# A relu moved forward on ScalarE, ahead of the lower sum that reads it, in a fused convolution and MLP kernel

## The chip, the cores and the metric

The kernel runs on one core of a Trainium2 chip. Its time is the device time of one execution in microseconds (us). Before the change it is 1008.81 us, the median of three runs (1006.14 to 1009.62).

## What is computed

The input x has 8 sequences of 4224 rows with 192 channels, all float32. First comes a causal convolution with 7 taps along the sequence; the 192 channels are 8 heads of 24, and each head has its own 7 weights, which are a softmax over the taps. Then an MLP block with a residual:

```python
w = softmax(weight)                        # (8 heads, 7 taps)
y = einsum('hk,bskhg->bshg', w, x_unfolded)   # y: (8, 4224, 192)
mu, var = mean(y), mean((y - mu) ** 2)     # over the 192 channels
yn = (y - mu) / sqrt(var + 1e-6) * g_ln
out = y + maximum(yn @ w_ch1, 0) @ w_ch2   # w_ch1: 192 x 768, w_ch2: 768 x 192
```

The kernel folds g_ln and the subtraction of the mean into the first weights, and since a positive factor passes through a relu, it multiplies by 1/sqrt(var) only after the second product.

## The kernel before

**Groups and stages.** The rows are cut into 18 groups. Groups 3 to 17 hold 16 rows on each of 128 partitions and are called mixed; a mixed group is one stage of the main loop. A stage does the first product with its relu (`up_mixed`) and then the second product (`down_fast`). Beside it, VectorE computes the convolution taps of the next group (`taps_of_next`, line 408), ScalarE the first two taps of the group after that (lines 383 and 394), and the output of the group before is scaled on ScalarE (`scale`, line 871, one row block j of 128 by 192 at a time) and added to memory by a DMA. The programs of the engines are in the order in which this file issues instructions; there is no reordering by a planner.

**A product in seven.** Both matrix products of a mixed group are done by Strassen's scheme in Winograd's form: the two operands are cut into quarters, and seven quarter products (with sums before and after) stand for eight. The hidden result has quarters c11, c12 (upper) and c21, c22 (lower).

**up_mixed.** The hidden dimension has 6 chunks of 128, three in each half. The pass is done for two sets of chunks: `one`, the small set (one chunk, index PAIR = 2), and `two` (two chunks, indices 0 and 1). Two sets of four PSUM banks, X and Y, take turns. In pass `two`, the line numbers and the order are these. `p.product` is TensorE (line 521). `p.evict` is ScalarE copying a bank set to the tile in SBUF, named room in the profile (line 616). `p.close(c, banks, part)` adds a bank set to a quarter: with a part, ScalarE copies the banks to the part (tiles parts_cs and parts_tb, or unused pieces of room) and a DMA from the GpSimd queue adds it (line 583, room<-parts_cs, room<-parts_tb, room<-room); without one, VectorE adds it directly (line 622). In the last stage all closes are VectorE's. `p.relu` is ScalarE in place (line 629).

The products accumulate: Y holds a11 b11, then s2 t0 on top of it (evicted as c21), then s1 b12, then s4 b22 (evicted as c12); X holds a12 b21, then s3 t1 (evicted as c22), then a22 t2, which `p.close(p.c21, X)` adds to c21 on VectorE. A product that follows an eviction or a close of the same banks waits for it.

**The lower sum.** `lower_sum` (line 767) is VectorE's in-place max(c21, 0) - c11, a first sum for the second product; it reads the relu of c11, chunk by chunk. It is called for chunk PAIR before `p.close(p.c21, X)`, and for the other two chunks after it.

**down_fast.** Seven products (line 791) of 36 matmuls, each recorded as two, in three column chunks c. The six banks are the next ones in turn, the four of X and two of Y. ScalarE copies finished chunks out (line 797), and after each copy it takes `behind` items from the list `work`: the relu of c22 of `one`, the scales, the two half relus of c22 of `two`, which the third product reads, and after them the first two taps of the group after next. `half_sum` (line 758) is VectorE's sums between the products. After them come the moments of the next group (line 439) and its sums (GpSimd lines 575 and 576, VectorE 578 and 579). In every second stage `root` then does the reciprocal square root on GpSimd (lines 457 to 470), in front of the next DMAs of the GpSimd queue.

Of the kernel before, what the change touches and what calls it, by code (L numbers as in the profile page):

```python
# [16 lines left out]
def kernel(  # L17
# [567 lines left out]
    def up_mixed(g, ahead):  # L585
# [9 lines left out]
        done = groups[g - 1][2]  # L595
# [40 lines left out]
        def act_scales(j1, j2):  # L636
            if not last:
                scale(g - 1, j1, j2)
# [7 lines left out]
        one, two = Pass(PAIR, FC, X, Y), Pass(0, PAIR, Y, X)  # L646
# [32 lines left out]
                add_to_out(g - 1, j1, j1 + HJ)  # L679
        p.product(Y, s2, p.t[0], False, False)  # L680
        p.evict(Y, p.c21)
        act_scales(1, 2)
        p.product(X, s3, p.t[1], True, False)
        p.evict(X, p.c22)
        act_scales(2, 3)
        p.product(Y, s1, p.b12, False, False)
        taps_of_next(2, 5)
        taps_of_next(5, 6, heads=(0, H // 2))
        p.close(p.c22, Y, rooms[1][:, 0:PAIR])
        act_scales(3, 4)  # L690
        p.product(X, a22, p.t[2], False)
        one.relu(one.c11)
        p.relu(p.c11)
        lower_sum(g, (PAIR,))
        p.close(p.c21, X)
# [11 lines left out]
        work = [lambda: one.relu(one.c22)]  # L707

        def scale_one(j):
            scale(g - 1, j, j + 1)  # L710
            if j == 7:
                add_to_out(g - 1, 0, 8)
            elif j == done - 1:
                add_to_out(g - 1, 8, done)

        if not last:
            work += [lambda j=j: scale_one(j) for j in range(4, done)]
        half = [lambda i=i: two.relu(two.c22[:, i : i + 1]) for i in range(PAIR)]
        return work[0:11] + half + work[11:]

    po = {}

# [146 lines left out]
    def scale(g, j1, j2):  # L869
        for j in range(j1, j2):  # L870
            nc.scalar.mul(ots[g][:, j, :], ots[g][:, j, :], rstd[g][:, j : j + 1])  # L871

    def add_to_out(g, j1, j2):
        if groups[g][0] is None:

            j1, j2 = (0, j2) if j2 == groups[g][2] else (0, 0)
        for ps, rows in rows_of_out(g, j1, j2) if j2 else ():
            nc.gpsimd.dma_start(  # L878
                out=rows, in_=ots[g][ps, j1:j2].rearrange("p j d -> p (j d)"), accum_op=ALU.add
            )  # L880
# [55 lines left out]
    def ahead(g):  # L936


        if results is not None:
            for half in range(2):  # L940
                finish_fast(g - 1, half, *results)
        yield

    for g in range(NG):
# [3 lines left out]
        if mixed:  # L948
            work = up_mixed(g, ahead(g))
        else:  # L950
            up(g)
# [73 lines left out]
```

## Time and profile before

| | busy us | share of the span |
|---|---|---|
| TensorE matmul | 958.6 | 95% |
| VectorE | 903.3 | 90% |
| ScalarE | 683.7 | 68% |
| GpSimd | 271.4 | 27% |

The profiled execution spans 1005.1 us; the granted TensorE clock is 0.996 of full speed. A stage in the middle, from the start of its second product to that of the next stage, takes 58.01 us (from 560.28 to 618.29); in it TensorE is busy for 55.95 us, VectorE 52.99, ScalarE 43.35 and GpSimd 12.45, and the DMA engines for a share of 0.77. The stage before, which has a `root` in front of its first product, takes 58.46.

The rows of the profile in the next parts are read as follows. PE is TensorE, DVE is VectorE, ACT is ScalarE and POOL is GpSimd. A timeline row has the start and the length in us, the engine, the line, the operation, the tile written and the tile read, the shapes and a count; what stands in brackets is how long the engine was idle before it, and what released it. Several like instructions can be merged into one row. Matmul ends are modelled.

### The profile page before, as it was taken

To read this page: it belongs to the slowest core of one execution; us is meant where nothing else is said; L and a number is where in the kernel's file an instruction comes from. 1 tells how busy PE (TensorE), PEld (TensorE's weight loads), DVE (VectorE), ACT (ScalarE), POOL (GpSimd) and SP (SyncE) were. 2 spreads that over 40 slices of the span, in tenths; PEclk is the share of its full clock that TensorE was granted. 3 is DMA by queue.
4 is the path that set the end of the run, shared out by engine and by line. 5 is a ranking of instruction groups with operands and counts; after the bars stand their busy time and mean duration, and the time that the engine had idled before them with its cause. 6 is when DMAs were issued, how large, how long until landed. Compare 5 with 4: busy or idle time off the path is not lost.

```text
span 1005.1 us, 38307 instructions
## 1 busy us (share of the span) xinstructions
PE 958.6 (95%) x17274; PEld 732.5 (73%) x17274; DVE 903.3 (90%) x1491; ACT 683.7 (68%) x1098; POOL 271.4 (27%) x383
## 2 busy tenths in 40 slices
PE   7999999999999999999999999999999899998997
PEld 6887586766869586776868677686867668595787
DVE  6999989979898998989899898989999798989757
ACT  5626577586877869586776958677695867775361
POOL 2004313513144221712135131523117121342200
PEclk9999999999999999999999999999999999999999
DMA  8252978478696877679787785878777796855031
GB/s 197 93 168 88 203 187 238 86 160 235 125 269 125 236 152 183 172 150 267 141 235 143 197 196 112 254 147 240 144 209 150 143 264 128 189 108 106 2 65 66
DMA packets 26386, 165.15 MB, mean 164 GB/s; under 512 B 3567, under 2 KB 4463, under 8 KB 18542
## 3 DMA queue, kind: packets, MB, share of 16 engines
q0 software_dynamic: 19120, 99.36, 50.6%
q1 hardware_dynamic: 6798, 63.34, 17.0%
q8 instruction: 135, 2.21, 0.9%
q14 instruction: 29, 0.24, 0.1%
q10 hardware_dynamic: 304, 0.00, 0.0%
HBM read 38.95 MB, written 50.33 MB: 89 GB/s over the span
## 4 chain that ended last, share of the span: by engine, by line
PE 58%; ACT 11%; DVE 10%; DMA 9%; POOL 6%; issue 5%; ACTq 0%; DVEq 0%; POOLq 0%
PE ps L521 31%; PE ps L791 21%; DVE room L758 7%; PE ps L738 5%; ACT room L629 5%; DMA room<-room 5%; ACT ot L871 4%; DMA room<-parts_cs 3%; DVE st L439 2%; ACT cs L797 2%; POOL d L457 2%; POOL d L467 1%; DMA xg<-in_x_dram 1%; ACT room L616 1%; POOL r L470 1%
## 5 line engine op out<-in xcount | busy, mean ns | idle before, releaser
L408 DVE SCALAR_TENSOR_TENSOR y<-xg,taps,y 128x384 f32<-128x384 f32 (+3 forms) x734 | 366.8, 578 | 0.2
L791 PE MATMUL ps<-room,w2sums 128*32 128x256 f32 (+1 forms) x4320 | 241.7, 377 | 8.1 <-ACT room L629 4.0
L521 PE MATMUL ps<-yt,w 32*128 32x256 f32 (+2 forms) x4104 | 238.6, 379 | 0.1
L616 ACT COPY room<-ps 128x1024 f32<-128x1024 f32 (+1 forms) x132 | 172.1, 1303 | 90.6 <-PE ps L521 80.6
L521 PEld LDWEIGHTS ps<-yt,w 32*128 32x128 f32 x4104 | 203.6, 185 | 27.7 <-issue 7.0
L791 PEld LDWEIGHTS ps<-room,w2sums 128*32 128x32 f32 x4320 | 146.4, 110 | 97.6 <-ACT room L629 17.1
L791 PE MATMUL ps<-room,w 128*32 128x256 f32 (+1 forms) x3240 | 181.6, 377 | 24.6 <-issue 21.7
L791 PEld LDWEIGHTS ps<-room,w 128*32 128x32 f32 x3240 | 111.8, 110 | 88.0 <-issue 32.0
L758 DVE TENSOR_TENSOR room<-room 128x1024 f32<-128x1024 f32 (+1 forms) x135 | 158.6, 1247 | 10.4 <-PE ps L791 10.4
L521 PE MATMUL ps<-ysums,w1sums 32*128 32x256 f32 x2160 | 123.8, 377 | 0.0
L521 PEld LDWEIGHTS ps<-ysums,w1sums 32*128 32x128 f32 x2160 | 110.5, 185 | 9.6 <-POOL v L458 1.8
L767 DVE SCALAR_TENSOR_TENSOR room<-room 128x1024 f32<-128x1024 f32 (+1 forms) x45 | 52.8, 1201 | 64.9 <-ACT room L629 63.5
L797 ACT COPY cs<-ps 128x256 f32<-128x256 f32 (+1 forms) x180 | 65.2, 365 | 65.7 <-PE ps L791 65.7
L871 ACT ACTIVATE ot<-ot,r 128x192 f32<-128x192 f32 x232 | 94.6, 455 | 0.0
L878 POOL DMA_DIRECT2D out_dram<-ot x40 | 34.3, 1079 | 209.6 <-ACT ot L871 131.1
L629 ACT ACTIVATE room<-room 128x1024 f32<-128x1024 f32 (+1 forms) x75 | 89.1, 1227 | 0.9 <-DMA room<-parts_cs 0.8
L383 ACT ACTIVATE y<-xg,taps 128x384 f32<-128x384 f32 (+3 forms) x141 | 74.1, 605 | 7.3 <-DMA out_dram<-y 6.9
L797 ACT COPY room<-ps 128x256 f32<-128x256 f32 (+1 forms) x90 | 33.4, 371 | 66.8 <-PE ps L791 66.8
L439 DVE BATCH_NORM_STATS2 st<-y 128x6 f32<-128x192 f32 x264 | 70.1, 341 | 0.0
L521 PE MATMUL ps<-yt,w1sums 32*128 32x256 f32 x1080 | 65.0, 379 | 2.3 <-ACT room L616 2.3
L521 PE MATMUL ps<-ysums,w 32*128 32x256 f32 x1080 | 64.8, 378 | 0.0
L394 ACT ACTIVATE tb<-xg,taps 128x384 f32<-128x384 f32 x112 | 60.3, 633 | 0.0
(103 smaller groups left out, 893.5 us busy)
## 6 DMA issues: line engine op xcount, KB each, us to landing
xg<-in_x_dram SPq DMA_DIRECT2D x15, 2112.0 KB, 15.9
out_dram<-ot POOLq DMA_DIRECT2D x29, 768.0 KB, 8.5
y<-tb POOLq DMA_DIRECT2D x28, 768.0 KB, 10.7
room<-room POOLq DMA_DIRECT2D x42, 512.0 KB, 5.7
out_dram<-y SPq DMA_DIRECT2D x13, 1536.0 KB, 8.0
room<-parts_cs POOLq DMA_DIRECT2D x14, 1024.0 KB, 8.5
room<-parts_tb POOLq DMA_DIRECT2D x14, 1024.0 KB, 6.9
xg<-in_x_dram SPq DMA_DIRECT2D x1, 1536.0 KB, 7.7
```

The costliest lines, as they stand in the source:

```text
L383: nc.scalar.mul(y[g][:, 0:n, cs], xg[g][:, 0:n, cs], taps[:, h, 0:1])
L394: nc.scalar.mul(tb[g][:, 0:n, cs], xg[g][:, 1 : 1 + n, cs], taps[:, h, 1:2])
L408: nc.vector.scalar_tensor_tensor(out=y[g][:, 0:n, cs], in0=t[:, k : k + n, cs], scalar=taps[:, h, k : k + 1], in1=y[g][:, 0:n, cs], op0=AL ...
L439: nc.vector.bn_stats(out=sums[g][:, j, :], in_=y[g][:, j, :])
L521: nc.tensor.matmul(banks[:, q, i * w : i * w + w], right[rows, c, P * i : P * i + P], left[rows, :, c, :], start=(first and c == 0 and i = ...
L616: nc.scalar.activation(dst, src, AF.Relu) if relu else nc.scalar.copy(dst, src)
L629: nc.scalar.activation(c, c, AF.Relu)
L758: nc.vector.tensor_tensor(a[:, *dst, f], a[:, *left, f], a[:, *right, f], op=op)
L767: nc.vector.scalar_tensor_tensor(out=a[:, 1, 0, f], in0=a[:, 1, 0, f], scalar=0.0, in1=a[:, 0, 0, f], op0=ALU.max, op1=ALU.subtract,)
L791: nc.tensor.matmul(dst[C * q : C * q + C, 0:w], right[:, f, C * c : C * c + C], left[:, f, q], start=(first and f == PAIR), stop=(f == PAI ...
L797: nc.scalar.copy(to[:, c], dst[:, 0:w].rearrange("p (j t) -> p j t", t=t))
L871: nc.scalar.mul(ots[g][:, j, :], ots[g][:, j, :], rstd[g][:, j : j + 1])
```

## The change

In `up_mixed`, the relu of the small set's upper left quarter, `one.relu(one.c11)`, moves from behind TensorE's last-but-one product to behind the c21 eviction of pass `two`, so that it is done before VectorE comes to the first lower sum. It takes the place of one scale of the group before; one more scale is taken out further down. These two scales (j = 2 and 3) are done in `down_fast` instead, at the head of its scales. There the half relus move from place 11 of the list to place 9, which is one copy sooner.

```diff
         p.product(Y, s2, p.t[0], False, False)
         p.evict(Y, p.c21)
-        act_scales(1, 2)
+        one.relu(one.c11)
         p.product(X, s3, p.t[1], True, False)
         p.evict(X, p.c22)
-        act_scales(2, 3)
+        act_scales(1, 2)
         p.product(Y, s1, p.b12, False, False)
         taps_of_next(2, 5)
         taps_of_next(5, 6, heads=(0, H // 2))
         p.close(p.c22, Y, rooms[1][:, 0:PAIR])
-        act_scales(3, 4)
         p.product(X, a22, p.t[2], False)
-        one.relu(one.c11)
         p.relu(p.c11)
         lower_sum(g, (PAIR,))
         p.close(p.c21, X)
...
         if not last:
-            work += [lambda j=j: scale_one(j) for j in range(4, done)]
+            work += [lambda j=j: scale_one(j) for j in range(2, done)]
         half = [lambda i=i: two.relu(two.c22[:, i : i + 1]) for i in range(PAIR)]
-        return work[0:11] + half + work[11:]
+        return work[0:9] + half + work[9:]
```

## The prediction

> **What bounds the kernel now.** First the busy shares of the page, which say whose time is being spent.
>
> ```profile
> PE 958.6 (95%) x17274; PEld 732.5 (73%) x17274; DVE 903.3 (90%) x1491; ACT 683.7 (68%) x1098; POOL 271.4 (27%) x383
> ```
>
> TensorE sets the pace, so a change counts only where TensorE stands still. Next, who waited for whom (waiter and line, what it waited for, total us, times, longest).
>
> ```profile
> DVE room L767 <- ACT room L629: 63.5, 14, 5.3
> PE ps L791 <- issue: 21.7, 14, 1.6
> PEld ps L791 <- ACT room L629: 17.1, 26, 0.8
> ```
>
> VectorE loses 63.5 us waiting for relus, in 14 stages: every mixed stage but the last. TensorE has 14 gaps of up to 1.6 us put down to "issue", so the profile names no cause. To find it I took one stage in order of time (start us, us, engine, line, operation), TensorE first.
>
> ```profile
> 611.33 2.77 PE L521 MATMUL ps<-yt,w1sums 32*128 32x256 f32 x48
> 613.91 2.77 PE L521 MATMUL ps<-ysums,w 32*128 32x256 f32 x48
> 618.29 4.09 PE L791 MATMUL ps<-room,w 128*32 128x256 f32 x72 [1.61 <-issue]
> 622.17 5.21 PE L791 MATMUL ps<-room,w2sums 128*32 128x256 f32 x88
> 627.69 3.23 PE L791 MATMUL ps<-room,w2sums 128*32 128x256 f32 x56 [0.31 <-ACT room L629]
> 630.74 4.07 PE L791 MATMUL ps<-room,w 128*32 128x256 f32 x72
> ```
>
> The first two rows are the last products of up_mixed, X with a22 and Y with s4; the rest are the first four of seven products of down_fast (72 records each), here P1 to P7. Starts tell more than the modelled ends. The step from 611.33 to 613.91 is 2.58, so P1 could have started at 616.49; it started at 618.29, 1.80 late. From P1 to P2 is 3.88; from P2 to P4 should be 7.76 and is 8.57, so the short wait inside P3 costs 0.81. It is in every mixed stage but the first and the last. Now VectorE and ScalarE in the same stretch.
>
> ```profile
> 595.36 14.87 DVE L408 SCALAR_TENSOR_TENSOR y<-xg,taps,y 128x384 f32<-128x384 f32 x28
> 614.77 1.22 DVE L767 SCALAR_TENSOR_TENSOR room<-room 128x1024 f32<-128x1024 f32 x1 [4.54 <-ACT room L629]
> 615.91 2.28 DVE L622 TENSOR_TENSOR room<-room,ps 128x2048 f32<-128x2048 f32 x1
> 618.29 2.36 DVE L767 SCALAR_TENSOR_TENSOR room<-room 128x1024 f32<-128x1024 f32 x2
> ```
>
> ```profile
> 606.39 1.87 ACT L616 COPY room<-ps 128x2048 f32<-128x2048 f32 x1 [0.37 <-PE ps L521]
> 608.15 0.46 ACT L871 ACTIVATE ot<-ot,r 128x192 f32<-128x192 f32 x1
> 609.02 1.87 ACT L616 COPY room<-ps 128x2048 f32<-128x2048 f32 x1 [0.41 <-ACT ot L871]
> 613.33 0.46 ACT L871 ACTIVATE ot<-ot,r 128x192 f32<-128x192 f32 x1
> 613.69 2.85 ACT L629 ACTIVATE room<-room 128x1024 f32<-128x1024 f32 x2
> 616.75 1.88 ACT L616 ACTIVATE room<-ps 128x2048 f32<-128x2048 f32 x1 [0.21 <-PE ps L521]
> ```
>
> VectorE is through with the taps at 610.23 and waits 4.54 for the first L629 relu (c11 of `one`) before the lower sum of L767. Behind that stands L622, close(c21, X), which reads bank set X; it ends at 615.91 + 2.28 = 618.19. P1 writes bank 0, which is in X, and starts at 618.29, 0.10 later. So I read the gap as ScalarE relu, lower sum, L622, TensorE. The last stage supports it: there the lower sum does not wait, and the gap is short and named (P1's start, and the L622 before it, which ends at 970.00):
>
> ```profile
> 970.14 2.89 PE L791 MATMUL ps<-room,w 128*32 128x176 f32 x72 [0.22 <-DVE room L622]
> 967.72 2.28 DVE L622 TENSOR_TENSOR room<-room,ps 128x2048 f32<-128x2048 f32 x1
> ```
>
> **What the Trainium skill says.** "Perfetto Trace Analysis", section "Per-instruction lifecycle: what the profiler-reported window actually captures", says ScalarE, VectorE and GpSimd are strict FIFOs and that TensorE's ends are estimated. The trace agrees: L622's product was over at 614.10, yet it ran at 615.91 behind L767; and I count TensorE's losses by starts. "PSUM — Partial Sum Buffer", section "Engine vs sequencer instructions", has the rule to guard PSUM by bank and quadrant; P1 waiting for the reader of X fits. "ScalarE: Activation LUTs", section "What ACT_TABLE_LOAD costs", gives 186 ns + 0.833 ns per element without pointer operands, an estimate of 1039 ns for 1024 elements; the trace has 1060 (median), which I use. "SBUF — State Buffer", section "Who interferes with whom", lets a VectorE instruction with two SBUF inputs block a GpSimd read. The trace agrees: GpSimd's L575 takes 1.84 at best and 3.44 in the median, beside L758.
>
> **The change part by part.**
>
> *1. Relu of c11 moved up.* It comes after the c21 eviction on ScalarE, in place of one scale: about 608.2 to 609.2. The lower sum then runs right after the taps, 610.3 to 611.5, and L622 waits for its product alone: 611.33 + 2.77 = 614.10, plus 0.14 (last stage: product end 964.57, L622 at 964.71) = 614.24, plus 2.28 = 616.52, plus 0.10: P1 at 616.62 instead of 618.29. Gain 1.67. VectorE's wait doesn't vanish: of 4.54 us, 2.8 become a wait for TensorE. In stages with a 1.45 gap (P1 at 560.28, product start 553.37 with an end of 556.24), P1 comes at 558.76, gain 1.52. The 21.7 us split into 9 of the first kind and 5 of the second: 9 x 1.67 + 5 x 1.52 = **22.6 us**.
>
> *2. What the early relu pushes.* Behind it on ScalarE stands the c22 eviction, and for that TensorE's X, a22 product waits. Before, it ran from 609.02; now the relu leaves it free at 608.15 + 0.96 = 609.12, ending at 610.99, while TensorE starts that product at 611.33. Cost 0, hidden by the Y, s1 product. The relu needs the first room<-room transfer. In stages after a `root`, GpSimd issues it late (540.65 in one) and transfers take 4.2 to 9.8 us: landing between 544.9 and 550.5, against a relu slot at 549.4. Even the slowest ends the relu at 551.46, and there the eviction waits for a later transfer until 551.45 anyway. Taken 0; upper end, were that later transfer early, 0.96 less the slack of 0.34 in 7 stages, 4.3 us.
>
> *3. Half relus one copy sooner, two more scales in down_fast.* The c12 eviction stays at 616.75 to 618.63, since TensorE sets it, so the first P1 copy starts near 618.6. ScalarE then runs without a pause at measured steps: copy 0.26, relu of c22 0.96, scale 0.35. Four copies (1.04), one relu, eight scales (2.8), half relu (0.96) and the second one's 1.06 end at 625.4. P3 reaches its last third at 616.62 + 7.77 + 0.86 = 625.25. So TensorE waits 0.16 instead of 0.81: 0.64 in 12 stages (the first had none; in g = 16 a wait for VectorE at 927.77, 2.63 long, swallows it) = **7.7 us**. The later scales delay taps and y<-tb by under 1 us; ScalarE's P5 copy came 1.6 us before P6 needed its bank, and y<-tb is read a stage later: 0.
>
> *4. What comes nearer.* (a) TensorE gains 0.64 inside P3, while VectorE's L758 sums, tied to L622, come only 0.2 earlier relative to P1. P5 needs three of them: 572.60 + 2 x 1.14 + 1.22 = 576.10 against 576.61 before; that slack goes. Estimate 0.05 in 13 stages, **0.7**. (b) In 7 stages the chain moments, root, room<-room, c22 eviction is late already (ScalarE waited up to 1.8 for it); TensorE's 0.45 lead is given back: **3.1** (ends 0 and 5). (c) In about 3 stages parts_cs lands so late (9.0 to 9.7 us) that the two-wide c11 relu cannot come sooner, so the c12 eviction and the half relus slip by 0.35: **1.0**.
>
> Sum: 22.6 + 7.7 - 0.7 - 3.1 - 1.0 = 25.5 us; 1008.8 - 25.5 = **983.3 us**.
>
> **The rivals.** *Only part one pays.* ScalarE starts down_fast no sooner, while TensorE does; if the copies slip, P3's wait stays at 0.8. If the transfers, in shorter stages, still take back the 4.8 of step 4, 22.6 - 4.8 = 17.8 is left, or 991; with the 4.3 of step 2 too, 995. For it: my ScalarE sum leaves 0.1 us. Against: every step is measured. *The gap is TensorE's own*, as "issue" reads literally; then only step 3 pays, 1001, and with 4 given back 1006. Against: the 0.10 after L622 in both kinds of stage. *Slower.* If the gap stays, the early relu adds its 0.6 over the scale to the c22 eviction in 14 stages (8.4) and TensorE waits for it: 1017. For it: ScalarE is in order and its relu depends on a transfer; against: 0.34 slack and an eviction that waits longer anyway. *Better.* If 4b costs nothing and the two later scales keep GpSimd's sums from slipping in ahead of L758 in g = 16 (2.6): 977.6.
>
> **How the numbers follow.** Forecast 0.62 (979 to 988), better 0.10, part one alone 0.17 (988 to 996), gap stays 0.06, slower 0.05. The range, 977 to 996, leaves out half of "better" and the last two. Faster is 0.62 + 0.10 + 0.17 + half of 0.06 = 0.92, same 0.03, slower 0.05.
>
> **What would show it.** The wait of L767 for L629 goes, and L622 waits about 2.8 us for its product instead; P1's gaps fall below 0.2; P2 to P4 takes 7.9; steady stages last 55.5 instead of 57.7, those after a root some 56.5. I am wrong if P1 still starts 1.5 late with L622 long over, if the X, a22 product waits for the c22 eviction in most stages, or if transfers take longer in the shorter stages (DMA is 0.77 busy in one).

## The result and the profile after

The changed kernel takes **981.34 us** (median of 4 runs, 979.82 to 983.43) against 1007.54 us; the ratio is **0.974**, with a 95% interval of 0.971 to 0.9769. The forecast was 983.3 us. On the chip of one of the later series of runs, where the kernel before takes 1011.23 us, the changed kernel takes 984.8, ratio 0.9736 (0.9714 to 0.9757).

The span of the profiled execution goes from 1005.1 to 978.0 us. The diff takes out two lines, so lines from about 691 on are two lower than before: L789 is the products of down_fast, L765 the lower sum, L756 the half sums. The busy shares of the page after:

```profile
PE 955.8 (98%) x17274; PEld 724.3 (74%) x17274; DVE 902.2 (92%) x1491; ACT 680.8 (70%) x1098; POOL 261.6 (27%) x383
```

All busy times are nearly the same; only TensorE's idle time has shrunk. From who waited for whom, after (waiter, what for, total us, times, longest):

```profile
DVE room L622 <- PE ps L521: 45.3, 17, 3.7
ACT room L629 <- DMA room<-parts_cs: 9.5, 8, 1.8
PEld ps L789 <- ACT room L629: 6.0, 16, 0.5
PEld ps L789 <- DVE room L622: 5.2, 15, 0.5
```

The 63.5 us that VectorE waited for the relu are gone, and so are TensorE's 14 gaps called "issue" in front of P1. In place of the former stands a wait of L622 for its own product, 45.3 us. A stage in order of time, after: TensorE, VectorE, ScalarE.

```profile
595.89 2.77 PE L521 MATMUL ps<-yt,w1sums 32*128 32x256 f32 x48
598.48 2.77 PE L521 MATMUL ps<-ysums,w 32*128 32x256 f32 x48
601.17 4.09 PE L789 MATMUL ps<-room,w 128*32 128x256 f32 x72
605.08 8.15 PE L789 MATMUL ps<-room,w2sums 128*32 128x256 f32 x144
612.97 4.15 PE L789 MATMUL ps<-room,w 128*32 128x256 f32 x72
```

```profile
580.54 14.87 DVE L408 SCALAR_TENSOR_TENSOR y<-xg,taps,y 128x384 f32<-128x384 f32 x28
595.33 1.22 DVE L765 SCALAR_TENSOR_TENSOR room<-room 128x1024 f32<-128x1024 f32 x1
598.79 2.29 DVE L622 TENSOR_TENSOR room<-room,ps 128x2048 f32<-128x2048 f32 x1 [2.25 <-PE ps L521]
```

```profile
590.95 1.87 ACT L616 COPY room<-ps 128x2048 f32<-128x2048 f32 x1 [0.37 <-PE ps L521]
592.71 1.06 ACT L629 ACTIVATE room<-room 128x1024 f32<-128x1024 f32 x1
593.67 1.86 ACT L616 COPY room<-ps 128x2048 f32<-128x2048 f32 x1
607.85 2.02 ACT L629 ACTIVATE room<-room 128x1024 f32<-128x1024 f32 x2
```

The relu (592.71) comes right after the c21 eviction, the lower sum (595.33) right after the taps, and L622 (598.79) 0.13 us after its product's modelled end (598.66). It is over at 601.08, and P1 starts at 601.17, 2.69 after the product before it: 0.10 late instead of 1.8. The half relus end at 609.87, and P2 to P4 takes 7.89.

To see where the time came from I added up TensorE's losses by starts, stage by stage, in the 14 mixed stages before the last. A product is late by what its start is behind the start of an earlier one plus the undisturbed step: 2.59 us for the X, a22 product and for P1, 3.885 from P4 to P5, 7.77 from P2 to P4 (under P3) and from P5 to P7 (under P7).

| late, us in all | before | after |
|---|---|---|
| P1 | 24.2 | 1.5 |
| P3 | 10.5 | 1.8 |
| P5 | 2.8 | 3.8 |
| P7 | 4.6 | 5.1 |
| X, a22 | 3.1 | 3.7 |

That is 22.7 + 8.7 - 1.0 - 0.5 - 0.6 = 29.3 us. The spans differ by 27.1. Of the rest, 1.2 us lies ahead of the first P1 (its lateness fell by 1.7, yet it starts only 0.44 sooner than before), some 0.4 in P1 to P2, 3.91 instead of 3.88, some 0.5 between P7 and the Y, s1 product of the next stage, and 0.1 behind the last P1.

### The profile page after: what moved, and what is told of

It is laid out like the page before. It is cut to its first block, busy times and chain, and to the rows that moved or that the text cites. A ratio compares the mean times of both kernels' runs of the same rounds, so it can differ in the third digit from the quotient of the medians.

```text
span 978.0 us, 38335 instructions
## 1 busy us (share of the span) xinstructions
PE 955.8 (98%) x17274; PEld 724.3 (74%) x17274; DVE 902.2 (92%) x1491; ACT 680.8 (70%) x1098; POOL 261.6 (27%) x383
## 4 chain that ended last, share of the span: by engine, by line
PE 72%; DVE 10%; DMA 6%; POOL 5%; ACT 4%; issue 2%; SPq 0%; ACTq 0%; DVEq 0%; POOLq 0%
PE ps L521 36%; PE ps L789 30%; DVE room L756 6%; PE ps L736 6%; DMA room<-room 5%; DVE st L439 2%; POOL d L457 1%; ACT room L616 1%; DMA xg<-in_x_dram 1%; ACT ot L869 1%; ACT room L629 1%; POOL d L467 1%; POOL r L470 1%; POOL room L583 1%; ACT cs L795 1%
## 5 line engine op out<-in xcount | busy, mean ns | idle before, releaser
L789 PE MATMUL ps<-room,w2sums 128*32 128x256 f32 (+1 forms) x4320 | 238.5, 377 | 4.5 <-DVE room L756 3.1
L789 PEld LDWEIGHTS ps<-room,w2sums 128*32 128x32 f32 x4320 | 142.5, 110 | 95.6 <-DVE room L756 6.7
L789 PE MATMUL ps<-room,w 128*32 128x256 f32 (+1 forms) x3240 | 182.4, 378 | 2.5 <-DVE room L756 2.4
L756 DVE TENSOR_TENSOR room<-room 128x1024 f32<-128x1024 f32 (+1 forms) x135 | 157.8, 1241 | 7.6 <-PE ps L789 7.6
L789 PEld LDWEIGHTS ps<-room,w 128*32 128x32 f32 x3240 | 107.4, 111 | 69.7 <-DVE room L622 5.2
L622 DVE TENSOR_TENSOR room<-room,ps 128x2048 f32<-128x2048 f32 (+1 forms) x20 | 42.5, 2128 | 45.5 <-PE ps L521 45.3
## 6 DMA issues: line engine op xcount, KB each, us to landing
y<-tb POOLq DMA_DIRECT2D x28, 768.0 KB, 10.7
```

The source lines that it names most:

```text
L756: nc.vector.tensor_tensor(a[:, *dst, f], a[:, *left, f], a[:, *right, f], op=op)
L789: nc.tensor.matmul(dst[C * q : C * q + C, 0:w], right[:, f, C * c : C * c + C], left[:, f, q], start=(first and f == PAIR), stop=(f == PAI ...
```

## The experiments

Each kernel ran beside the kernel before on the same chip; the ratio is to that, with its interval. On the chips of these runs the kernel before takes 1011 to 1012 us, not 1007.5, so absolute forecasts are to be read some 4 us higher.

| run | us | ratio (interval) | P1 | P3 | P5 | P7 | X, a22 |
|---|---|---|---|---|---|---|---|
| relu_only | 995.24 | 0.9825 (0.9803 to 0.9847) | 1.5 | 14.3 | 2.5 | 4.6 | 5.8 |
| half_only | 1010.73 | 0.9989 (0.9976 to 1.0002) | 24.1 | 0.0 | 3.4 | 9.7 | 8.9 |
| order_only | 1041.72 | 1.0295 (1.0276 to 1.0315) | 1.7 | 14.0 | 3.8 | 37.4 | 4.7 |
| order_and_half | 1045.05 | 1.0323 (1.03 to 1.0345) | 1.9 | 1.6 | 14.6 | 38.8 | 7.5 |
| order_half_guard | 989.5 | 0.9774 (0.9759 to 0.9788) | 1.6 | 2.1 | 10.7 | 0.8 | 8.2 |
| half_guard | 999.75 | 0.9888 (0.9862 to 0.9914) | 23.9 | 0.0 | 0.2 | 0.3 | 9.0 |
| relu_twice | 991.3 | 0.9792 (0.9776 to 0.9808) | 1.5 | 1.5 | 3.4 | 4.3 | 11.8 |
| after_again | 984.8 | 0.9736 (0.9714 to 0.9757) | 1.5 | 1.7 | 3.7 | 4.3 | 6.9 |
| after_guard | 979.24 | 0.9674 (0.9659 to 0.9689) | 1.5 | 1.8 | 0.6 | 1.0 | 7.5 |
| guard_two_ends | 979.82 | 0.9682 (0.9658 to 0.9706) | 1.5 | 1.9 | 0.5 | 1.1 | 8.8 |
| root_two | 975.99 | 0.964 (0.9624 to 0.9657) | 1.5 | 1.6 | 3.6 | 2.9 | 0.6 |
| guard_and_root_two | 970.36 | 0.9589 (0.9563 to 0.9616) | 1.5 | 1.6 | 0.2 | 0.0 | 0.0 |

The last five columns are the losses of the table above, for each run. They count how late a product starts, not how long it then takes. That matters because TensorE's granted clock falls to 0.50 for 3.41 us at a time in some traces, each time at a long stop of TensorE. Such a stretch costs some 1.7 us. Between the first mixed stage and the last product there are two in the traces before, after, relu_only, half_only, relu_twice and after_again, eleven in order_only, ten in order_and_half (one of them twice as long), and none in root_two and the kernels with a guard; order_only, below, shows one.

### The two halves of the change, each alone

relu_only moves the relu and leaves all four scales in up_mixed and the half relus in their place:

```diff
         p.evict(Y, p.c21)
-        act_scales(1, 2)
+        one.relu(one.c11)
         p.product(X, s3, p.t[1], True, False)
         p.evict(X, p.c22)
-        act_scales(2, 3)
+        act_scales(1, 2)
...
-        act_scales(3, 4)
+        act_scales(2, 4)
         p.product(X, a22, p.t[2], False)
-        one.relu(one.c11)
         p.relu(p.c11)
```

> The kernel before with only the relu of c11 moved behind the c21 eviction; all four scales stay in up_mixed (one place later each), and the half relus stay at place 11. Theory: P1's lateness goes as in the full change (22.7 us), the wait inside P3 grows to about 1.2 us: about 990 us, like the reordering on VectorE alone. Rival, the early relu delays the c22 eviction and TensorE's X, a22 product waits for it: over 1000 us.

It went so: P1 on time, 1.07 us late at P3 in the steady stages instead of 0.8, ratio 0.9825 (990 of 1007.5 is 0.983). So the relu's move alone carries P1's gain, and it turns part of it into a longer wait at P3. half_only moves the half relus alone; what the two later scales do by themselves no run shows:

```diff
-        return work[0:11] + half + work[11:]
+        return work[0:9] + half + work[9:]
```

> The kernel before with only the half relus of c22 moved from place 11 to place 9 of the list. Theory: the wait inside P3 (0.8 us by starts, 12 to 13 stages) goes, P1's lateness of 1.6 to 1.8 stays: about 8 to 9 us less, 998.5 us. Rival, the wait inside P3 is taken up again by the sums before P5: no change, 1007 us.

A miss. P3 is on time, which is worth 10.5 us, and nothing is gained: the ratio's interval holds 1. Beside the trace of the kernel before, P5 and P7 are 5.8 us later in all, and the X, a22 product is 5.8 us later too. In one stage of half_only, VectorE's half sums, GpSimd's sums, and TensorE at P7 and at X, a22:

```profile
635.13 12.44 DVE L758 TENSOR_TENSOR room<-room 128x1024 f32<-128x1024 f32 x9
```

```profile
643.97 2.51 POOL L575 TENSOR_TENSOR ysums<-yt 128x768 f32<-128x768 f32 x1
646.56 2.70 POOL L576 TENSOR_TENSOR ysums<-ysums,yt 128x768 f32<-128x768 f32 x1
```

```profile
647.72 4.09 PE L791 MATMUL ps<-room,w 128*32 128x256 f32 x72 [1.10 <-DVE room L758]
...
676.43 2.87 PE L521 MATMUL ps<-yt,w1sums 32*128 32x256 f32 x48 [1.84 <-ACT room L616]
```

The nine half sums take 12.44 us instead of 10.3: the last of them takes 3.40 (from 644.18) while GpSimd's sums run. This is so in four of the twelve stages between g = 3 and g = 16; in the other eight the nine take 10.27. P7 waits for it, the moments and root come 2 us later, and so, perhaps, does the c22 eviction behind root's transfers. Whether this is the cause is tested by half_guard below. The twenty runs scatter from 1005.83 to 1014.86 us, and the trace is of one that took 1013.64.

### The same gap, closed on VectorE

order_only doesn't touch ScalarE. It lets L622 go ahead of the lower sum:

```diff
-        lower_sum(g, (PAIR,))
         p.close(p.c21, X)
+        lower_sum(g, (PAIR,))
```

> The kernel before with one edit on VectorE alone: close(c21, X) is called ahead of the first lower sum; ScalarE's order, the relu of c11 and the scales stay as they were. If P1's gap is L622 standing behind the lower sum that waits for the relu, L622 runs at its product's end and P1's lateness falls from 1.6 to 1.8 to about 0.1 in 14 stages (22.7 us), though the relu is as late as ever. The half relus keep their place while TensorE comes earlier, so the wait inside P3 grows from 0.8 to about 1.2 us in 12 stages (4.8 us given back): about 990 us. If the gap is TensorE's own (the literal 'issue') or hangs on the relu's time itself, nothing moves: 1007 us, within 3.

P1's lateness fell to 0.12 with the relu as late as ever. This decides what "issue" stood for: the gap is L622 behind a lower sum that waits. But the kernel became 3% slower than before. One stage of order_only, VectorE, GpSimd and TensorE:

```profile
598.08 14.53 DVE L758 TENSOR_TENSOR room<-room 128x1024 f32<-128x1024 f32 x9
```

```profile
606.27 2.51 POOL L575 TENSOR_TENSOR ysums<-yt 128x768 f32<-128x768 f32 x1
608.86 2.67 POOL L576 TENSOR_TENSOR ysums<-ysums,yt 128x768 f32<-128x768 f32 x1
```

```profile
601.72 7.95 PE L791 MATMUL ps<-room,w2sums 128*32 128x256 f32 x144
612.76 5.78 PE L791 MATMUL ps<-room,w 128*32 128x256 f32 x72 [3.09 <-DVE room L758]
```

The lower sum behind L622 puts one more instruction, 1.1 us, in front of the half sums, so that they start 13.0 us after P1 instead of 12.3, and GpSimd's sums come to lie beside the last two: nine take 14.53 us. P7 is 3.3 late in eleven stages, and in ten of these it then takes 5.7 instead of 4.0 us.

The second loss is not a wait for data: the last half sum is over at 612.61, before P7 starts. It is TensorE's clock. The rows show a stretch each before, within and behind P7: its start and end, its length, the busy time and count of TensorE, its weight loads, VectorE, ScalarE and GpSimd, then the granted clock, the DMA share and GB/s.

```profile
605.00:609.50 4.50, 4.50 (x88) 2.56 (x80) 4.50 (x2) 1.24 (x4) 4.26 (x4) 1.00 0.99 254
613.60:616.80 3.20, 3.20 (x37) 1.97 (x30) 3.20 (x14) 0.37 (x1) 0.00 (x0) 0.50 1.05 215
618.50:621.00 2.50, 2.50 (x51) 2.33 (x48) 2.47 (x4) 1.26 (x2) 0.00 (x0) 1.00 0.00 0
```

In the middle stretch TensorE gets through 37 matmuls in 3.20 us, at the end 51 in 2.50. Against the kernel before, P7's late starts cost 33 us more, and the slow stretches behind them some 15 us more. order_and_half adds the half relus at place 9:

> The kernel before with the reordering on VectorE alone and the half relus at place 9; the relu of c11 is not moved and no scale is moved. Theory: both losses go by other means than the relu's move, P1 0.1 late and the wait inside P3 about 0.1: equal to the changed kernel within 3 us, 981 us. Rival, the relu's early place has a worth of its own (the two-wide relu of c11 and the c12 eviction come sooner): over 986 us.

A miss for the same reasons: P1 and P3 are on time, but P7 is late by 3.4 in eleven stages, with TensorE at half clock behind most of these stops, and the ratio is 1.0323.

### GpSimd kept away from the half sums

The guard is one small GpSimd instruction ahead of its sums. It reads the last half sum and so waits for it:

```diff
             moments(g + 1)
+            nc.gpsimd.tensor_copy(after_sums, a[:, 0, 1, FC - 1, 0, 0, 0:1])
             sums = sums_of_y(g + 1, nc.gpsimd)
```

order_half_guard is order_and_half with it.

> The kernel before with the reordering on VectorE, the half relus at place 9 and the same GpSimd copy ahead of L575; the relu of c11 stays late. Theory: the 34 to 62 us that the reordering alone lost against the forecast were GpSimd's sums slipping in between the half sums, which run one VectorE instruction later there; with the copy the half sums are back at 10.3 us for nine, P7's lateness of 3.3 goes in 11 stages, and 0.8 us stays at P5 in each: 984 us, ratio 0.974. Rival, the reordering itself costs the time (VectorE being an instruction later): above the kernel before, ratio over 1.0.

```profile
621.78 10.27 DVE L759 TENSOR_TENSOR room<-room 128x1024 f32<-128x1024 f32 x9
```

One instruction turns 1.0323 into 0.9774. The half sums are back at 10.27, P7's loss goes from 38.8 to 0.8, no stretch at half clock is left, and 0.83 remains at P5, as said. The rival, that the reordering itself costs the time, is out. (The 34 us in the forecast should be some 48: order_only's 990 is 994 on its chip, and it took 1041.72.) The ratio is a little above the 0.974 forecast; X, a22 loses 8.2 there, which may be part of it. half_guard is half_only with the guard.

> The kernel before with the half relus at place 9 and the GpSimd copy ahead of L575; the relu of c11, the scales and VectorE's order as before. Theory: the half relus alone gained nothing because GpSimd's sums came to lie between the half sums (a half sum of 3.4 us) and root and the transfers came later; with the copy P5 and P7 are on time, P3 is on time, and P1's lateness of 1.6 to 1.8 stays: ratio about 0.986, against 0.999 for the half relus alone. Rival, the gain at P3 cannot be kept while L622 is late: 0.995 or more.

0.9888, with the expected 0.986 just below the interval. P3 stays on time, P5 and P7 are now on time too, P1 is as late as before. This confirms what took half_only's gain back at P5 and P7, but not all of the gain here is the half relus' own, as the guard takes away losses that the kernel before has as well (some 7 us at P5 and P7). For X, a22 it confirms nothing: 9.0 us are lost there with the half sums back at 10.27, so the long half sums do not explain half_only's 8.9. No trace of the kernel before was taken beside these runs, and how much of that loss is the change's stays open. after_guard is the changed kernel with the guard.

> The changed kernel with one GpSimd instruction more in each stage but the last: a one-element copy that reads the last of the nine half sums (L756 of the changed kernel), ahead of GpSimd's own sums (L575), so that these cannot start while VectorE's half sums run. Theory: where L575 slips in between two half sums, one of them takes 3.3 us instead of 1.2 (both read two SBUF operands), and that made P7 late in g = 3 and P5 and P7 in g = 16: 9 us together. With the copy both go and no stage gets longer, since L576 still ends before VectorE asks for it: 972 us, ratio to the kernel before 0.965. Rival, the long half sums have another cause, or VectorE now waits for L576: 981 us or more.

In g = 16 the half sums of the changed kernel and of after_guard, and the P5 that waits for them in the changed kernel:

```profile
893.88 13.52 DVE L756 TENSOR_TENSOR room<-room 128x1024 f32<-128x1024 f32 x9
```

```profile
900.64 9.66 PE L789 MATMUL ps<-room,w2sums 128*32 128x256 f32 x144 [3.08 <-DVE room L756]
```

```profile
900.14 10.27 DVE L757 TENSOR_TENSOR room<-room 128x1024 f32<-128x1024 f32 x9
910.32 1.08 DVE L821 TENSOR_TENSOR cs<-cs,ps 128x256 f32<-128x256 f32 x3
```

P5 and P7 are on time in g = 3 and g = 16. What the table has at P7 for g = 16 of the changed kernel (1.71) is no wait, but P5 at half clock behind its stop: P5 and P6 take 9.66 us, and with the guard that stretch is gone as well. Of 9 us forecast, about 6.8 came (0.974 of 1012.35 is 986.0). I put the difference down to X, a22, and guard_two_ends was to show it, with the guard in g = 3 and 16 alone.

> The changed kernel with the GpSimd copy ahead of L575 in stages g = 3 and g = 16 alone, the two where a half sum took 3.3 us. Theory: the 9 us of P5 and P7 there go, and the 3.8 us go too that the copy in every stage cost at the X, a22 products after a root (GpSimd was later there): ratio 0.966 or a little less. Rival, the copy in every stage lost nothing by itself, the difference being the transfers' scatter: 0.967, like the copy in every stage.

The rival was right: 0.9682, the same as with the guard everywhere, and X, a22 loses 8.8. So no cost of the guard shows there. after_again, without any guard, loses 6.9 at X, a22, against 3.7 in the first run:

> The changed kernel itself, to stand beside the other three on their chip: ratio 0.974 to the kernel before.

The lateness after a root thus differs between two traces of the same program. They are from different series of runs; whether the chip makes the difference, one trace from each doesn't tell.

### Root, and the slack behind the early relu

root_two takes away one of three Newton steps:

```diff
-        for _ in range(3):
+        for _ in range(2):
```

> The changed kernel with two Newton steps in root instead of three (the last correction of the reciprocal square root is left out): GpSimd is free for the room<-room transfers about 2 us sooner in the 7 stages with a root. Theory: the late X, a22 products there (3.7 us by starts in the changed kernel) are the chain moments, root, room<-room, c22 eviction, and go: 3 us less, 978 us, ratio 0.971. Rival, the transfers themselves are slow there whenever they start: no change, 0.974.

In a stage after a root, GpSimd's issue of the three transfers and TensorE's X, a22 product, first in the changed kernel (P1 at 489.40), then in root_two (P1 at 490.61):

```profile
527.91 2.41 POOL L583 DMA_DIRECT2D room<-room  x3
```

```profile
540.38 2.87 PE L521 MATMUL ps<-yt,w1sums 32*128 32x256 f32 x48 [0.70 <-ACT room L616]
```

```profile
526.75 2.41 POOL L583 DMA_DIRECT2D room<-room  x3
```

```profile
540.72 2.77 PE L521 MATMUL ps<-yt,w1sums 32*128 32x256 f32 x48
```

The transfers are issued 36.1 us after P1 instead of 38.5, and the wait for the c22 eviction is gone; X, a22 loses 0.6 in all stages together, and 10 us are saved (986.0 to 975.99) instead of the 3 expected. The mechanism held; the size was taken from the first trace's 3.7, while after_again has 6.9 to give. The spans of after_again and root_two differ by 9.8 us. Of these, 6.3 are X, a22's lateness, and 1.7 a stretch at half clock from 210.20 on in after_again, behind a stop of 1.93 us for the c22 eviction, which root_two does not have. Another 1.4 are P7's, nearly all in g = 16: TensorE stops in front of P5 for nearly as long there (2.96 us against 3.10), but no half clock follows. That root brought this about is not shown. relu_twice doubles the early relu:

```diff
         p.evict(Y, p.c21)
         one.relu(one.c11)
+        one.relu(one.c11)
```

> The changed kernel with the early relu of c11 done twice (the second leaves the values as they are): 0.96 us more on ScalarE in front of the c22 eviction. Theory: the eviction had 0.3 us to spare before TensorE's X, a22 product, so that product comes 0.66 late in the stages without a late transfer, and little is added where the eviction waited for a transfer anyway: 9 x 0.66 = 6 us more than the changed kernel, ratio 0.980. Rival (the relu stands on TensorE's path already): the whole 0.96 in 14 stages, 13.4 us more, ratio 0.987. If the eviction has more room than I think: no change, 0.974.

```profile
599.59 2.15 ACT L629 ACTIVATE room<-room 128x1024 f32<-128x1024 f32 x2
601.64 1.85 ACT L616 COPY room<-ps 128x2048 f32<-128x2048 f32 x1
```

```profile
603.54 2.87 PE L521 MATMUL ps<-yt,w1sums 32*128 32x256 f32 x48 [0.61 <-ACT room L616]
```

Now the eviction ends at 603.49 and the product waits for it: 0.78 late in nearly every stage. Against after_again's 984.8 that is 6.5 us (5.7 by the ratios, as the chips differ), near the 6 forecast. So the single relu fits, and hardly more would. The last kernel joins the guard and the shorter root:

> The changed kernel with the GpSimd copy in every stage and two Newton steps in root instead of three (the last correction of the reciprocal square root is left out). Theory: the late X, a22 products (7.5 us by starts with the copy alone) go, and so do the 8 us of P5 and P7: 967 to 970 us on this chip, ratio 0.956, faster than either alone. Rival, with both the transfers limit the stages: 0.964, like two steps alone.

970.36 us, ratio 0.9589, the fastest here. Steady stages last 55.4 us, with a root or without, and of the tallied losses little is left but 0.11 at P1 and at P3. It does one correction of the reciprocal square root less, which is a choice of precision and not of order; after_guard, at 0.9674, changes no arithmetic.

## Why the prediction was right

**Relu moved up**: 22.6 us forecast, 22.7 measured at P1. P1's lateness was said to fall to 0.12 and is 0.11. That the gap was L622 and not TensorE's own is shown by order_only, which closes it another way.

**What the early relu pushes**: 0 forecast. In the stages without a root in front, X, a22 is 0.00 late. relu_twice shows the slack that this rested on.

**Half relus, with the two later scales**: 7.7 forecast, 8.7 measured. The wait left is 0.11 where 0.16 was worked out, and g = 16, which I had left out, gained at P3 too.

**VectorE's sums before P5**: 0.7 forecast; P5 lost 1.0 more, but 0.45 of it in g = 16, and most stages lost nothing. The half sums do start without a wait, and fit.

**The chain behind root**: 3.1 forecast, 0.6 measured in this pair of traces, the one term that was clearly mis-sized; after_again's 6.9 has no trace of the kernel before beside it. I took TensorE's lead of 0.45 us as lost at all 7 stages. TensorE is late there in four of them before (0.6 to 1.1 us) and in five after (0.3 to 1.2). In the trace that chain has come forward as well: in the two stages with P1 at 501.82 before and 489.40 after, the transfers are issued 38.8 and 38.5 us after P1, and X, a22 starts 51.6 and 51.0 after it. The chain itself is real (root_two). **Late parts_cs**: 1.0 forecast; P3's loss rose by 0.1 in the two or three stages concerned.

The two large terms are right in mechanism and size. That the total came so close (25.5 forecast, 27.1 between the spans) is in part luck: root and parts_cs cost 3.4 us less than forecast, P3 gave 1.0 more, and some 2.2 us were lost in places that the forecast did not look at.

**The better case** counted on GpSimd's sums leaving the half sums of g = 16 alone. They did not: 13.52 us there, P5 3.3 late. The long half sums, which I had seen in g = 3 and g = 16 only, I took for an exception. half_only and order_only show that other stages stand close to it. The full change avoided it there: GpSimd's L575 takes 2.5 us (median) beside 3.4 before, as it now comes when the last half sum is nearly done. Nothing in my working promised that, so it was luck; I priced the later transfer of y<-tb at nothing and did not ask what the GpSimd sums behind it would meet.

## What to carry to other kernels

A short gap with no named cause is best read by what ends just before it: the same 0.10 us behind L622 in stages of two kinds, and a last stage without the wait, were enough. An instruction that waits holds back all that stands behind it on its engine, so ask for the last one in that queue, not for the one that waits. And before moving anything by a microsecond, look at which pairs of operations on VectorE and GpSimd would then overlap: half_only gave back 5.8 of the 10.5 us won at P3 that way, and a reordering that closed the gap cost 3%, until one guard instruction kept the two apart. Where TensorE is made to stop for 3 us, look at its granted clock behind the stop as well: in order_only the slow stretches added about half as much again to what the late starts cost.

## What the runs showed of the hardware

A half sum on VectorE that normally takes 1.2 us took up to 3.9 when a GpSimd sum lay beside it (order_only), while the additions from PSUM and the moments did not get longer beside the same GpSimd sums (1.08 for three and 4.26 for sixteen in after_guard, 1.07 and 4.24 in order_only, where no GpSimd sum lay beside them). This agrees with the Trainium skill, "SBUF — State Buffer", section "Who interferes with whom": two SBUF inputs on VectorE contend with a GpSimd read. Which of the two is held varied: in the kernel before GpSimd mostly lost (L575 3.44 in the median against 1.84 at best) and the half sums kept their 10.3; in order_only VectorE mostly lost. GpSimd came during the eighth of nine half sums, 0.6 us after its start in the kernel before and 0.3 in order_only. But in one stage of order_only (half sums from 901.35) GpSimd came at the same 0.27 us and was held itself, for 3.78 us, while the half sums kept 10.27. So the moment of arrival does not decide alone; what does is left open.

After a long stop TensorE can run at half its clock for a while. In the fourteen traces, between the first mixed stage and the last product, each stretch at a granted clock of 0.50 lies at a stop of TensorE of 1.93 us or more (by its modelled ends), and begins between 0.9 us before and 1.2 us after its restart. All but one last 3.41 us. No shorter stop has one, such as the repeated 1.61 us in front of P1 in the kernel before. Not every long stop has one either: stops of 2.38 and 2.96 us in root_two have none.
